# A gated linear-attention layer and its feed-forward on one core: the hand-kept list of 1,629 steps is written in another order

## The chip, the core and the metric

The kernel runs on 1 core of one Trainium2 chip. The measure is the device time of one execution in microseconds (us). The core has five instruction streams: TensorE (PE, whose weight loads are shown apart as PEld), VectorE (DVE), ScalarE (ACT), GpSimd (POOL) and SyncE (SP, which only issues transfers here). Each takes its own instructions strictly in the order written, and waits for the others through semaphores.

## What is computed

The first half is a recurrent attention with an exponential input gate and a forget gate, over 4 batches, 8 heads, 768 positions and 40 values a head. The second half is a two-layer feed-forward with a piecewise activation, over all 3,072 positions, 320 wide with 2,048 hidden units.

```python
for t in range(S):
    m_new = np.maximum(f_gate[:, :, t] + m, i_gate[:, :, t])
    f_stab = np.exp(f_gate[:, :, t] + m - m_new)
    i_stab = np.exp(i_gate[:, :, t] - m_new)
    C = f_stab * C + i_stab * einsum('bhd,bhe->bhde', vt, kt)
    n = f_stab * n + i_stab * kt
    h_tilde = einsum('bhde,bhe->bhd', C, qt)
    denom = np.maximum(np.abs(einsum('bhd,bhd->bh', n, qt)), 1.0)
    y[:, :, t] = sigmoid(o_gate[:, :, t]) * h_tilde / denom
h = y @ w_in
g = np.where(h >= 1, h, np.where(h <= -1, 0.0, (h + 1) ** 2 / 4))
out = g @ w_out
```

All inputs and the output are 32-bit floats. The matrices of the feed-forward are split into a high and a low part, so that several products of narrower words make up one exact enough product.

## The kernel before

Time is cut into 6 chunks of 128 positions. With 4 batches that makes 24 attention pieces, numbered n = 0 to 23. The feed-forward works on 6 groups j of 512 positions (four pieces each) and 16 slices of 128 hidden units, so on 96 blocks numbered 16j + slice. A block can start when all four pieces of its group are done.

Everything after the set-up is driven by one string, `STEPS`, near the top of the file. A loop goes through its words and issues the instructions of each. The words that the text uses are:

- `fi`, `fb`, `qk.n`, `v.n`, `A.n`, `W.k`, `og.c` load (SP issues): gates, queries and keys, values, cumulated decays, weight block k, output gates of a chunk.
- `score.n` (PE, then two DVE products into the decay tile `Abc`), `prep.n` (a POOL selection, then two times four ACT exponentials on `Abc`), `carry.n` (the state `C`), `main.n` (the rest of a piece: products, normalization, `y`, a transpose by PE, and then the split copies `xh`, on ACT, and `xl`, on DVE).
- `mm.x`, `relu.x`, `max.x`, `gh.x`, `gl.x`, `out.x`/`outh.x`/`outl.x`: the eight products of block x (PE), its activation (two ACT instructions `r`), the limit (DVE), the high part (ACT), the low part (DVE) and the second product (PE).
- `w.k`: the next part of the conversion of weight block k. The weights arrive as 64-bit words, and W.0 to W.15 are alternately blocks of the first matrix (`win`, even k) and of the second (`ow`, odd k). The word `w.k` stands five to seven times in the list, and each time one instruction of the block is issued: two on ACT (`mg<-wraw`, then `win<-wraw` or `ow<-wraw`), three on DVE (`mg<-mg`, then `win<-wraw` or `ow<-wraw`, then `win<-mg,win` or `ow<-mg,ow`). Even blocks go on with a cast `wh<-win` on ACT and the rest `wl<-win,wh` on DVE. For odd blocks the word `so.i` does the same later (`oh<-ow` on ACT).
- `hot.k`: k products on zeros, to keep PE busy; `sig.c`: the sigmoid of a chunk, which needs another table on ACT (ACT_TABLE_LOAD before and after).

The conversion of a block begins like this; `mg` is one buffer for all blocks, and so is the `win` tile of the even ones:

```python
mg = stage.tile([P, n], F32, name="mg", bufs=1)
nc.scalar.activation(mg, hi.bitcast(F32), AF.Abs, scale=65536.0)
yield
out = new().rearrange("p k f -> p (k f)").bitcast(I32)
...
nc.vector.tensor_scalar_max(mg, mg, TINY)
yield
...
nc.vector.scalar_tensor_tensor(out=out, in0=mg.bitcast(I32), scalar=3, in1=out,
```

So the first ACT instruction of block k+1 waits until the fifth instruction of block k (the third on DVE, `ow<-mg,ow` or `win<-mg,win`) has read `mg`. The blocks of the first feed-forward group (x = 0 to 15) need the weights in step with their numbers: `mm.x` needs both parts of W.k with k = x or x - 1, whichever is even.

The list decides the order of every engine's instructions, and with it what stands ahead of what; nothing reorders them later. Two words in it, `--` and `++`, close the buffers of the gates and of the weight conversion and open others in their place.

Of the kernel before, what the change touches and what calls it, by code (L numbers as in the profile page):

```python
# [48 lines left out]
    "fi.0 mask.1 fb.0 W.0 vv.0 mask.0 hot.2 sums.0 mask.3 qk.1 add.1 hot.2 add.0 qk.2 w.0 w.0 bmax.0 id.0 dec.1.0 "  # L49
    "dec.1.1 dec.0.0 score.1 qk.3 gtail.0 hot.2 hot.2 bmax.0 gex.0 score.1 mask.2 w.0 qk.0 add.2 dec.2.0 dec.2.1 "  # L50
    "vv.2 add.3 w.0 v.4 dec.3.1 v1.1 dec.3.0 score.1 og.0 W.1 dec.0.1 score.2 main.1 score.0 bsum.0 bsum.0 bsum.0 "
    "w.0 score.3 score.2 score.2 one.0 score.0 v.1 score.0 v1.2 btail.0 w.0 v1.0 sig.0 main.1 btail.0 hot.4 "
    "btail.0 btail.0 w.0 v1.3 main.0 score.3 v.0 main.0 W.2 hot.2 exps.0 main.0 main.1 main.2 hot.2 hot.2 qn.5 A.4 "
    "score.3 v2.4 main.2 main.2 main.0 w.1 v2.1 qk.4 main.0 w.1 w.1 cs.0 main.3 main.1 main.2 main.0 W.3 v.5 "
    "carry.4 main.3 main.3 hot.2 v2.0 qn.4 main.1 w.1 decs.0 main.1 v.2 w.1 carry.1 main.3 A.5 A.6 main.2 w.2 "
    "carry.0 main.2 main.3 main.3 prep.4 carry.0 w.2 v1.4 w.2 mm.0 mm.1 prep.4 v2.5 w.2 W.4 w.2 -- prep.4 qk.6 "
    "carry.1 w.2 score.4 w.3 w.2 w.3 relu.1 main.4 main.4 mm.3 v2.2 prep.5 qk.5 w.3 carry.5 score.4 W.5 relu.0 W.6 "
    "relu.3 w.3 score.4 carry.5 max.1 prep.6 w.3 mm.2 main.5 relu.2 w.4 max.0 max.2 main.4 carry.2 decs.0 main.4 "
    "out.0 v.3 og.1 v.6 max.3 w.4 qn.6 v1.5 prep.6 carry.4 prep.5 w.4 so.0 W.7 w.4 w.5 main.5 w.4 out.1 A.7 "
    "score.5 w.4 carry.5 carry.2 score.5 w.5 main.4 w.5 w.4 v.7 score.6 prep.6 out.2 mm.4 carry.4 w.5 prep.5 "  # L60
    "score.6 w.6 w.6 sig.1 mm.5 w.5 score.5 w.6 v1.6 W.8 main.5 w.6 v2.6 relu.5 w.6 w.6 main.6 v2.3 W.9 out.3 w.7 "
    "qn.7 score.6 qk.7 carry.5 prep.7 main.5 relu.4 main.4 max.5 w.7 w.6 prep.7 main.6 main.6 W.10 carry.6 w.8 "
    "max.4 main.6 v1.7 qn.8 carry.6 mm.6 carry.3 W.11 w.8 w.7 relu.6 w.7 w.7 mm.7 relu.7 out.4 carry.4 carry.3 "
    "main.7 main.5 W.12 w.8 w.8 W.13 main.5 w.8 v2.7 max.6 main.4 max.7 main.7 out.5 main.4 w.9 w.9 w.8 prep.7 v.8 "
    "main.4 W.14 w.9 w.9 score.7 carry.6 out.6 w.10 carry.6 so.1 w.9 v.9 w.10 w.8 mm.9 score.7 relu.9 w.10 w.10 "
    "mm.8 qn.9 score.7 w.10 w.10 w.11 w.11 relu.8 main.6 main.7 max.9 w.10 w.12 A.8 w.11 mm.10 w.11 w.11 qk.8 A.9 "
    "W.15 main.6 max.8 w.12 w.12 mm.11 relu.11 w.12 so.5 w.12 carry.7 out.7 w.12 main.7 w.13 so.5 w.12 qk.9 mm.13 "
    "w.13 max.11 relu.10 w.13 w.13 main.5 gh.11 w.13 w.14 max.10 main.5 gl.11 v2.8 carry.7 gh.10 main.7 out.8 "
    "mm.12 w.14 A.11 w.14 prep.8 relu.13 w.14 relu.12 prep.8 gl.10 main.5 out.9 v1.8 prep.8 max.12 w.14 prep.9 "
    "w.14 max.13 outh.10.0.1 outh.10.2.3 outl.10 main.6 so.6 main.7 w.15 main.6 score.8 w.15 score.8 outh.11.0.1 "  # L70
    "outh.11.2.3 outl.11 score.8 w.14 w.15 w.15 gh.12 so.6 qn.11 w.15 ++ gh.13 main.8 main.8 main.6 mm.14 prep.9 "
    "qk.10 relu.14 mm.15 og.2 main.7 gl.12 so.2 main.8 gl.13 outh.12.2.3 qk.10 main.7 relu.15 main.8 max.14 main.9 "
    "lg.0 main.7 gh.14 A.10 outh.12.0.1 so.7 outl.12 stack.10 so.1 outh.13.2.3 main.8 outh.13.0.1 carry.7 mm.17 "
    "main.8 outl.13 so.7 qk.11 max.15 mm.16 main.8 main.9 relu.17 gh.15 prep.9 v1.9 score.9 max.17 gl.14 gl.15 "
    "stack.10 relu.16 main.8 gh.17 outh.14.2.3 outh.14.0.1 prep.10 outl.14 mm.19 outh.15.0.1 stack.10 sig.2 "
    "carry.7 gl.17 main.8 qn.10 mm.20 outh.15.2.3 max.16 gh.16 outl.15 main.9 relu.19 prep.10 stack.10 mm.18 "
    "carry.8 score.9 main.8 gl.16 score.9 sto.0.2 sto.0.0 mm.22 max.19 carry.8 relu.20 main.9 v.10 score.10 so.0 "
    "relu.18 sto.0.3 main.8 main.9 max.20 v2.9 sto.0.1 qk.11 main.9 mm.21 main.10 A.12 score.10 max.18 so.2 "
    "prep.11 relu.22 main.10 so.4 main.9 main.8 outh.16.2.3 outh.16.0.1 outl.16 prep.10 carry.8 so.3 qn.13 "
    "outh.17.0.1 gh.18 max.22 outh.17.2.3 main.8 prep.11 stack.11 gh.20 score.10 gh.19 v1.10 outl.17 so.4 carry.9 "  # L80
    "gl.18 relu.21 outh.18.2.3 outh.18.0.1 carry.8 carry.9 stack.11 carry.9 v.11 main.10 outl.18 gl.20 v2.10 qk.12 "
    "mm.25 main.10 gl.19 relu.25 outh.19.0.1 main.9 outh.19.2.3 mm.23 outl.19 max.21 outh.20.2.3 gh.22 so.3 "
    "outh.20.0.1 prep.12 main.10 max.25 gh.21 gl.21 carry.9 mm.24 carry.10 stack.11 outl.20 main.9 stack.12 "
    "relu.23 prep.12 relu.24 main.9 prep.11 main.10 outh.21.2.3 v.12 qk.12 stack.11 qn.12 max.23 outh.21.0.1 "
    "carry.10 outl.21 score.11 main.11 A.13 v2.11 main.10 score.11 mm.27 max.24 outh.22.0.1 stack.12 main.10 "
    "score.11 prep.12 gh.24 main.10 gh.23 gl.22 relu.27 mm.31 v1.11 mm.28 relu.31 g5.5 gl.23 main.11 main.10 qk.14 "
    "main.11 outh.22.2.3 main.11 qk.13 gl.24 gh.25 carry.10 mm.26 outl.22 outh.23.0.1 max.31 main.10 relu.26 "
    "max.27 outh.23.2.3 stack.12 main.11 main.12 stack.14 prep.13 outl.23 outh.24.2.3 outh.24.0.1 A.14 main.11 "
    "gl.25 outl.24 max.26 main.9 main.12 qk.13 og.3 stack.14 relu.28 max.28 main.11 carry.10 main.11 outh.25.0.1 "
    "mm.29 stack.12 v1.12 gh.27 gh.26 main.9 outh.25.2.3 gl.27 main.12 carry.11 v.13 relu.29 gl.26 main.9 main.11 "  # L90
    "outl.25 stack.13 outh.26.2.3 mm.30 v.14 prep.13 main.12 outh.26.0.1 A.15 gh.28 carry.11 score.12 main.11 "
    "outl.26 v2.12 relu.30 max.29 gl.28 qk.15 score.12 outh.27.2.3 score.12 main.12 outh.27.0.1 main.11 carry.12 "
    "outl.27 max.30 main.10 outh.28.2.3 prep.13 carry.11 outh.28.0.1 main.10 main.11 stack.13 qk.15 stack.13 "
    "main.13 main.12 outl.28 main.11 gh.29 mm.35 main.13 relu.35 qn.14 gh.30 gh.31 mm.34 carry.11 main.12 stack.13 "
    "gl.30 carry.12 v1.13 gl.29 outh.29.0.1 mm.32 outh.29.2.3 relu.34 outl.29 outh.30.0.1 main.13 max.35 gh.35 "
    "main.13 relu.32 main.12 stack.15 v2.13 max.32 outh.30.2.3 max.34 outl.30 gh.32 outh.31.2.3 gl.31 score.13 "
    "mm.33 score.13 mm.39 score.13 main.12 outh.31.0.1 outl.31 relu.33 qk.14 stack.15 gl.32 prep.14 g5.5 gl.35 "
    "carry.12 main.13 prep.14 carry.12 max.33 carry.13 mm.36 mm.38 main.13 carry.13 sto.1.3 relu.39 g5.5 sto.1.0 "
    "relu.36 main.14 qk.16 A.16 gh.33 main.13 max.36 carry.13 v.15 sig.3 mm.41 stack.14 prep.15 outh.32.0.1 "
    "outh.32.2.3 sto.1.1 g5.5 gl.33 relu.41 outl.32 main.13 qn.15 max.39 mm.37 sto.1.2 stack.15 outh.33.0.1 "  # L100
    "stack.14 outh.33.2.3 main.13 gh.34 qk.16 gh.39 main.13 stack.15 relu.37 outl.33 gl.34 main.12 v1.14 gh.36 "
    "outh.34.0.1 gl.39 max.41 qk.17 prep.14 outh.34.2.3 main.14 outl.34 outh.35.0.1 qn.17 score.14 max.37 qn.16 "
    "outh.35.2.3 qk.17 score.14 gl.36 stack.16 v.16 A.17 relu.38 outl.35 carry.13 main.14 g5.5 score.14 gh.37 "
    "outh.36.2.3 mm.43 outh.36.0.1 main.15 v2.14 carry.14 mm.40 outl.36 v2.15 outh.37.2.3 stack.16 max.38 main.14 "
    "score.15 gh.38 outh.37.0.1 gl.37 outl.37 prep.15 main.12 carry.14 main.14 main.15 outh.38.2.3 g5.5 score.15 "
    "relu.40 carry.14 outh.38.0.1 gl.38 A.18 main.14 prep.15 max.40 qn.19 outl.38 prep.16 v.17 stack.16 qk.18 "
    "outh.39.2.3 g5.5 outh.39.0.1 main.12 main.13 main.12 score.15 stack.17 v1.15 stack.17 main.14 main.13 gh.40 "
# [922 lines left out]
```

## Time and profile before

| | |
|---|---|
| time before, median of 3 runs | 471.26 us (469.88 to 471.52) |
| span of the profiled execution, from first to last instruction | 467.8 us |
| the profiled execution's own time beside its span | not recorded; the median of the runs is 3.5 us above the span |
| PE busy | 458.4 us, 98% of the span, 3312 matmuls |
| DVE, ACT, POOL busy | 359.8 us (77%), 326.0 us (70%), 150.5 us (32%) |
| chain of work that ended last | PE 94%, DVE 2%, DMA 1% |
| transfers | 60.60 MB, mean 130 GB/s |

The table is read as follows: PE has hardly any idle time in this execution, while DVE and ACT have a quarter to a third over the whole span, but not in each stage of it. A matmul is shown as busy until its modelled end, and consecutive ones overlap.

### The profile page before, as it was taken

Reading aid. Unit: us, or ns where it says so; the run is one execution under the profiler, and the core shown is the slowest. Engines: PE = TensorE matmul, PEld = TensorE weight load, DVE = VectorE, ACT = ScalarE, POOL = GpSimd, SP = SyncE. Lnnn points to the kernel's source line nnn. Section 1 sums busy time; section 2 is a strip of 40 time slices with the busy share of each in tenths; the row PEclk is TensorE's granted clock in tenths of the full one; section 3 lists DMA queues with packets and bytes.
Section 4 is the critical chain, followed back from the end, with each engine's and each line's share of the span. In section 5 each row is a group of like instructions: output and inputs, shape, how many; then the busy total and the mean of one; then the engine's idle time right before and its main releaser. Section 6 shows DMA issues by size and latency. Waiting matters only on the chain.

```text
span 467.8 us, 8768 instructions
## 1 busy us (share of the span) xinstructions
PE 458.4 (98%) x3312; PEld 407.1 (87%) x3312; DVE 359.8 (77%) x651; ACT 326.0 (70%) x587; POOL 150.5 (32%) x153
## 2 busy tenths in 40 slices
PE   6999999999999999999999999999999999999997
PEld 3888787788899999889899989999899989888996
DVE  5888888999989889698998988887578875343342
ACT  3578898998987556588675986766596735544561
POOL 2265042133454554332543433452243240000000
PEclk9999999999999999999999999999999999999999
DMA  6899955656452534526234654424533000001001
GB/s 219 281 288 324 331 177 186 202 194 160 116 177 70 175 89 154 138 80 202 76 117 149 169 150 128 128 70 138 157 100 115 2 1 1 1 0 57 0 1 56
DMA packets 24552, 60.60 MB, mean 130 GB/s; under 512 B 2599, under 2 KB 12607, under 8 KB 24511
## 3 DMA queue, kind: packets, MB, share of 16 engines
q1 hardware_dynamic: 24223, 59.81, 41.8%
q8 instruction: 26, 0.43, 0.4%
q10 hardware_dynamic: 288, 0.25, 0.2%
q14 instruction: 15, 0.12, 0.1%
HBM read 55.96 MB, written 4.01 MB: 128 GB/s over the span
## 4 chain that ended last, share of the span: by engine, by line
PE 94%; DVE 2%; DMA 1%; SPq 1%; ACT 1%; issue 0%; DVEq 0%
PE ps L191 94%; DMA raw<-in_qk 1%; DVE gl L191 1%; SPq L191 1%; DVE ow L191 1%; ACT r L191 0%; DVE wl L191 0%; DVE Abc L191 0%; ACT oh L191 0%; DVE z L191 0%; DVE r L191 0%; ACT xh L191 0%; SPq L188 0%; DVE y L191 0%; DVE xh L191 0%
## 5 line engine op out<-in xcount | busy, mean ns | idle before, releaser
L191 PE MATMUL ps<-oh,gh 128*128 128x320 f32 x344 | 105.6, 317 | 0.0
L191 ACT ACTIVATE r<-ps,half 128x512 f32<-128x512 f32 x96 | 65.6, 684 | 56.1 <-PE ps L191 41.6
L191 PE MATMUL ps<-ow,gh 128*128 128x320 f32 x344 | 103.0, 309 | 0.0
L191 PE MATMUL ps<-xh,wh 128*128 128x512 f32 x288 | 100.6, 403 | 0.8 <-ACT xh L191 0.8
L191 PE MATMUL ps<-xh,wl 128*128 128x512 f32 x288 | 98.3, 395 | 0.3 <-DVE wl L191 0.3
L191 DVE TENSOR_TENSOR gl<-r,gh 128x512 fp32r<-128x512 f32 x86 | 65.7, 770 | 38.2 <-ACT gh L191 35.6
L191 DVE SCALAR_TENSOR_TENSOR r<-ps,r 128x512 f32<-128x512 f32 x96 | 65.1, 684 | 24.1 <-ACT r L191 23.9
L191 ACT CAST gh<-r 128x512 fp32r<-128x512 f32 x86 | 52.0, 613 | 38.9 <-PE ps L191 32.2
L191 PE MATMUL ps<-oh,gl 128*128 128x320 f32 x344 | 66.0, 312 | 1.0 <-DVE gl L191 1.0
L191 PEld LDWEIGHTS ps<-oh,gh 128*128 128x128 f32 x344 | 64.6, 188 | 2.2 <-ACT o L191 0.2
L191 PEld LDWEIGHTS ps<-ow,gh 128*128 128x128 f32 x344 | 64.8, 188 | 1.8
L191 PEld LDWEIGHTS ps<-xh,wl 128*128 128x128 f32 x288 | 54.0, 188 | 13.5 <-DVE wl L191 0.7
L191 ACT ACTIVATE r<-r 128x512 f32<-128x512 f32 x96 | 60.7, 633 | 3.0
L191 PE MATMUL ps<-xl,wh 128*128 128x512 f32 x192 | 60.3, 395 | 0.0
L191 PEld LDWEIGHTS ps<-xh,wh 128*128 128x128 f32 x288 | 50.3, 188 | 8.2 <-ACT xh L191 1.0
L191 PEld LDWEIGHTS ps<-oh,gl 128*128 128x128 f32 x344 | 54.3, 188 | 2.5 <-DVE gl L191 1.2
L191 POOL TENSOR_TENSOR v<-vk,G 128x328 f32<-128x328 f32 x36 | 30.7, 855 | 70.3 <-PE ps L191 40.5
L191 ACT ACTIVATE Abc<-Abc,nA 128x128 f32<-128x128 f32 x160 | 50.4, 390 | 3.4 <-POOL Abc L191 3.3
L191 POOL TENSOR_TENSOR y<-y,z 128x320 f32<-128x320 f32 x24 | 22.9, 957 | 77.3 <-DVE y L191 75.0
L191 POOL TENSOR_TENSOR m<-m 128x1024 bf16<-128x1024 f32 x16 | 32.9, 2053 | 40.8 <-DVE m L191 38.6
L191 PEld LDWEIGHTS ps<-xl,wh 128*128 128x128 f32 x192 | 36.0, 188 | 8.8
L191 DVE SCALAR_TENSOR_TENSOR stk<-raw,ident,qs 120x1024 fp32r<-120x1024 f32 x28 | 37.0, 1326 | 1.1 <-ACT raw L191 1.0
(146 smaller groups left out, 711.1 us busy)
## 6 DMA issues: line engine op xcount, KB each, us to landing
qs<-in_qs SPq DMA_DIRECT2D x28, 480.0 KB
Abc<-a_d SPq DMA_DIRECT2D x20, 512.0 KB
vk<-in_vk SPq DMA_DIRECT2D x20, 324.0 KB
wraw<-in_w_in SPq DMA_DIRECT2D x8, 768.0 KB
wraw<-in_w_out SPq DMA_DIRECT2D x8, 640.0 KB
sig<-in_og SPq DMA_DIRECT2D x6, 640.0 KB
qn<-in_qn SPq DMA_DIRECT2D x20, 180.0 KB
raw<-in_qk SPq DMA_DIRECT2D x20, 160.0 KB
```

The costliest lines, as they stand in the source:

```text
L191: r = getattr(self.engine, name)(*args, **kwargs)
```

## The change

`STEPS` is replaced by another order of the same 1,629 words. Every word stands in both lists equally often, so operations, buffers, pools and inputs are the same; the marks `--` and `++` stand at other places in the list (words 139 and 407 before, 115 and 418 after). Two lines of each list, from the stretch in which W.1 to W.4 are converted:

```diff
-    "carry.0 main.2 main.3 main.3 prep.4 carry.0 w.2 v1.4 w.2 mm.0 mm.1 prep.4 v2.5 w.2 W.4 w.2 -- prep.4 qk.6 "
-    "carry.1 w.2 score.4 w.3 w.2 w.3 relu.1 main.4 main.4 mm.3 v2.2 prep.5 qk.5 w.3 carry.5 score.4 W.5 relu.0 W.6 "
+    "decs.0 so.0 A.6 carry.1 w.2 w.2 v2.0 A.5 qk.5 carry.0 carry.0 w.2 w.2 W.5 mm.0 mm.1 w.2 w.2 prep.4 relu.0 v2.5 "
+    "main.4 main.4 v2.2 w.2 score.4 prep.4 score.4 qk.6 main.5 main.5 W.6 max.0 carry.5 w.3 w.3 prep.4 score.4 "
```

The first place is ACT's row from the first transposed copies (`xh`) to the conversion of W.3. `mg` and `win` at 128x768 are W.2's two parts, `wh` its cast; `mg` and `ow` at 128x640 are W.3's; `r` is an activation and `Abc` an exponential of `prep.4`. Before:

```order
L191 CAST xh<-ps 128x3x128
L191 ACTIVATE mg<-wraw 128x768
L191 CAST xh<-ps 128x3x128
L191 ACTIVATE win<-wraw 128x768
L191 ACTIVATE Abc<-Abc,nA 128x128 x8
L191 CAST wh<-win 128x3x256
L191 ACTIVATE mg<-wraw 128x640
L191 ACTIVATE ow<-wraw 128x640
L191 ACTIVATE r<-ps,half 128x512
L191 ACTIVATE r<-r 128x512
```

The same place after the change (`oh` is `so.0`, the cast of W.1):

```order
L190 CAST oh<-ow 128x640
L190 ACTIVATE mg<-wraw 128x768
L190 ACTIVATE win<-wraw 128x768
L190 CAST wh<-win 128x3x256
L190 ACTIVATE r<-ps,half 128x512
L190 ACTIVATE r<-r 128x512
L190 ACTIVATE Abc<-Abc,nA 128x128 x4
L190 ACTIVATE mg<-wraw 128x640
L190 ACTIVATE ow<-wraw 128x640
L190 ACTIVATE Abc<-Abc,nA 128x128 x4
```

Eight exponentials stood between `win` and `wh` and now nothing does; `oh` now stands ahead of W.2, and an activation and four exponentials stand ahead of W.3.

The second place is ACT's row at the conversion of W.12 (the parts at 128x768) and the start of W.13's (at 128x640). Before:

```order
L191 ACTIVATE mg<-wraw 128x768
L191 ACTIVATE win<-wraw 128x768
L191 ACTIVATE r<-ps,half 128x512
L191 ACTIVATE r<-r 128x512
L191 CAST oh<-ow 128x640
L191 CAST wh<-win 128x3x256
L191 ACTIVATE mg<-wraw 128x640
L191 ACTIVATE ow<-wraw 128x640
```

After:

```order
L190 ACTIVATE mg<-wraw 128x768
L190 ACTIVATE win<-wraw 128x768
L190 CAST oh<-ow 128x640
L190 ACTIVATE r<-ps,half 128x512
L190 ACTIVATE r<-r 128x512
L190 CAST xh<-ps 128x3x128
L190 ACTIVATE r<-ps,half 128x512
L190 ACTIVATE r<-r 128x512
L190 CAST wh<-win 128x3x256
L190 ACTIVATE mg<-wraw 128x640
```

One more activation and one `xh` copy stand ahead of W.12's cast, and so ahead of W.13.

## Rows read from the trace of the kernel before

**Rows 1.** The page: the span, and PE's busy time, its share and instructions.

```profile
span 467.8 us, 8768 instructions
PE 458.4 (98%) x3312; PEld 407.1 (87%) x3312; DVE 359.8 (77%) x651; ACT 326.0 (70%) x587; POOL 150.5 (32%) x153
```

**Rows 2.** PE's waits: line, waited for, us in total, times, longest.

```profile
PE ps L191 <- DMA raw<-in_qk: 1.5, 2, 0.9
PE ps L191 <- DVE gl L191: 1.0, 1, 1.0
PE ps L191 <- ACT xh L191: 0.8, 1, 0.8
PE ps L191 <- DVE wl L191: 0.3, 1, 0.3
```

**Rows 3.** Busy time by engine (instructions), 26 to 116 us; then clock, DMA share, GB/s.

```profile
26.00:116.00 90.00, 88.91 (x540) 73.67 (x539) 80.47 (x146) 77.90 (x139) 30.70 (x32) 1.00 0.74 233
```

**Rows 4.** Instructions on tile mg: min/median/max ns, first and last start us.

```profile
L191 ACT ACTIVATE mg<-wraw x15: 787/813/925, 25.1 to 103.2; 128x640 f32<-128x640 f32 x8, 128x768 f32<-128x768 f32 x7
...
L191 DVE SCALAR_TENSOR_TENSOR ow<-mg,ow x8: 803/826/1281, 29.7 to 106.4; 128x640 int32<-128x640 int32 x8
```

**Rows 5.** ACT, 26 to 116 us by form: busy us, mean ns | idle before.

```profile
L191 ACT ACTIVATE Abc<-Abc,nA 128x128 f32<-128x128 f32 x44 | 13.6, 389 | 0.0
L191 ACT ACTIVATE r<-ps,half 128x512 f32<-128x512 f32 x17 | 11.5, 674 | 4.4 <-PE ps L191 4.4
L191 ACT ACTIVATE r<-r 128x512 f32<-128x512 f32 x17 | 10.7, 631 | 0.5
L191 ACT ACTIVATE win<-wraw 128x768 uint16<-128x768 uint16 x7 | 7.6, 1089 | 0.0
L191 ACT ACTIVATE ow<-wraw 128x640 uint16<-128x640 uint16 x8 | 7.4, 926 | 0.0
L191 ACT ACTIVATE mg<-wraw 128x768 f32<-128x768 f32 x7 | 6.3, 907 | 3.9 <-DVE ow L191 3.8
L191 ACT CAST wh<-win 128x768 fp32r<-128x768 f32 x7 | 5.8, 824 | 0.8 <-DVE win L191 0.8
L191 ACT ACTIVATE mg<-wraw 128x640 f32<-128x640 f32 x7 | 5.6, 796 | 0.7 <-DVE win L191 0.7
L191 ACT CAST oh<-ow 128x640 fp32r<-128x640 f32 x6 | 4.3, 718 | 0.0
L191 ACT CAST xh<-ps 128x384 fp32r<-128x384 f32 x8 | 3.8, 472 | 1.7 <-PE ps L191 1.6
...
L191 ACT ACT_TABLE_LOAD x2 | 2.6, 1283 | 0.0
L191 ACT ACTIVATE sig<-sig 128x1280 f32<-128x1280 f32 x1 | 1.3, 1270 | 0.0
```

**Rows 6.** DVE, the same window and columns: the parts of the weight conversion.

```profile
L191 DVE SCALAR_TENSOR_TENSOR ow<-mg,ow 128x640 int32<-128x640 int32 x8 | 7.0, 879 | 0.3
...
L191 DVE SCALAR_TENSOR_TENSOR win<-mg,win 128x768 int32<-128x768 int32 x7 | 6.7, 955 | 0.3
L191 DVE TENSOR_SCALAR win<-wraw 128x768 uint16<-128x768 uint16 x7 | 5.4, 775 | 0.0
L191 DVE TENSOR_SCALAR mg<-mg 128x768 f32<-128x768 f32 x7 | 4.8, 689 | 0.4 <-ACT mg L191 0.4
L191 DVE TENSOR_SCALAR ow<-wraw 128x640 uint16<-128x640 uint16 x8 | 4.6, 569 | 0.0
...
L191 DVE TENSOR_SCALAR mg<-mg 128x640 f32<-128x640 f32 x8 | 4.2, 527 | 0.0
```

**Rows 7.** ACT in order of time from 25 us: start, length [idle before].

```profile
25.89 0.48 ACT L191 CAST xh<-ps 128x384 fp32r<-128x384 f32 x1
26.27 0.93 ACT L191 ACTIVATE ow<-wraw 128x640 uint16<-128x640 uint16 x1
```

**Rows 8.** SP's issue of transfers in order of time: start, length of the issue.

```profile
1.19 0.70 SPq L191 DMA_DIRECT2D fi_r<-in_fi  x1
```

223 rows, old and new, of the table STEPS are left out of this document.

## The prediction

> **What bounds the kernel now.** I read the page's busy times first. PE is busy for 458.4 of 467.8 us [rows 1], and the reader is to see that a reordering alone cannot take away more than the 9.4 us that are left. Next I read PE's waits. Of those on other engines and on transfers, four groups stand out: 1.5 us for the first queries and keys, 1.0 for a `gl`, 0.8 for an `xh` and 0.3 for a `wl` [rows 2]. That is 3.6 us in all, the most that a better order has to win in the places that the profile names. So the old list runs near PE's pace, and the question is what the new one makes PE wait for.
>
> Then I looked for a stage in which the other engines have little to spare. From 26 to 116 us DVE is busy for 80.5 and ACT for 77.9 of 90 us, with the clock of PE at full (1.00) [rows 3]. This is where the weights are converted. The view of the tile `mg` shows the conversion as one thread: W.1's first instruction starts at 25.1 us, W.15's fifth at 106.4 and takes about 0.8, so it ends at 107.2 [rows 4]. It lasts 82.1 us. Since `mg` is one buffer, no block may begin before the fifth part of the block ahead, so the parts form a serial chain that goes from ACT to DVE and back. ACT stood still 3.8 us for that reason [rows 5].
>
> Taken alone, the parts of one block last, on the even blocks, 0.907 + 1.089 + 0.689 + 0.775 + 0.955 = 4.4 us, on the odd ones 0.796 + 0.926 + 0.527 + 0.569 + 0.879 = 3.7 us [rows 5, 6]. For 7 even and 8 odd blocks this is 60.4 of the 82.1 us. Only 21.7 us of other work and waiting lay on that thread in the old order.
>
> **The change, part by part.** *The conversion.* The first pair of rows of the order shows the pattern. Before, W.2's `win` and `wh` had eight exponentials between them, so ACT worked while DVE did W.2's three parts. After, nothing stands between them and ACT waits. The work that filled the gap (an activation, four exponentials, the cast `oh`) now stands ahead of the next block's first part, so it adds to the thread. The second pair shows the same at W.12, with one activation more ahead of the cast and of W.13.
>
> I followed the new order back from the last use of the converted weights through whatever stands immediately ahead in its engine's row, or through the producer when that ends later. Of the 75 parts of W.1 to W.15, 57 are on this chain (beside the others an engine has longer work): the first ACT part 7 times odd and 5 even, the second 7 and 5, DVE's first 8 and 3, second 8 and 3, third 8 and 3. With the means of rows 5 and 6 that is 5.57 + 4.54 + 6.48 + 5.45 + 4.22 + 2.07 + 4.55 + 2.33 + 7.03 + 2.87 = 45.1 us. To it come:
> - 6 casts `wh` at 0.824 and 3 `oh` at 0.718: 7.1 us [rows 5].
> - 8 activations of two instructions, 0.674 + 0.631: 10.4 us [rows 5].
> - 20 exponentials. They overlap, and 13.6 us of busy time over 44 makes 0.309 each: 6.2 us [rows 5].
> - `sig.1` with its two table loads, 1.270 + 2 × 1.283: 3.8 us [rows 5].
> - One `xh` copy, 0.5 us [rows 5].
> - 26 further DVE instructions of the attention. The window's DVE time without the conversion's six forms is 80.47 - 32.7 = 47.8 us over 146 - 45 = 101 instructions, 0.473 each: 12.3 us [rows 3, 6].
> - 7 on POOL (selections and products) at 30.70 / 32 = 0.96: 6.7 us [rows 3].
>
> The sum is 92.1 us. Neighbours on one engine overlap: an `xh` copy from 25.89 lasts 0.48, and the next instruction starts at 26.27, 0.10 early [rows 7]. Over some 95 such neighbours I take off 0.065 each (an estimate between nothing and the 0.10 of that pair), 6.2 us; for some 35 passes from engine to engine I add 0.035 each, an estimate, 1.2 us. That leaves 87.1 us against the 82.1 before: **+5.0 us**. The bounds are 92.1 (no overlap at all, +10.0) and, with the full 0.10 and free passes, 82.6 (+0.5).
>
> What hides this? Nothing, I think: PE waits for `wl` and `xh` in just this stage already [rows 2], so a thread that ends later moves the first products of W.12 and W.14, then the second group's blocks, by as much. Behind it PE has no idle time in which to catch up; what it loses stays lost.
>
> At one point of this sum the notes on the chip put another price. In the rows the table load takes 1.283 us, and the two instruction forms that follow such loads show 0.0 us of idle time ahead [rows 5]. The Trainium skill (ScalarE: Activation LUTs, What ACT_TABLE_LOAD costs) states for each switch the same 1.283 us and a drain of about 1.38 us on top. By it the two switches on the chain would cost 2.8 us more and the sum would be +7.8; the trace does not show the drain.
>
> *The start.* The new list issues `fb`'s two loads ahead of `fi`, so the first gate arithmetic comes later by their issue, of which one takes 0.70 us [rows 8]; the queries and keys for the first products are ahead of the weights instead of behind them. PE lost 1.5 us there before [rows 2]. The two work against each other, and I take 0, with bounds of -1.5 (that wait is gone, and the gates' lateness stays covered by products on zeros and masks) and +1.4 (two issues of that length, with nothing else to do).
>
> *The middle and the end.* From about 116 us on, the new order keeps PE's operations and mixes them otherwise. DVE and ACT have slack there, and before, PE's named wait in that part was 1.0 us for a `gl` [rows 2]. I take 0, between -1.0 (that wait goes) and +2.0 (two more like it). The last four stores change places, which I take as 0: the same copies and issues stand behind the last product.
>
> The sum is +5.0 us: the span goes to 472.8 and, with the 3.5 us that the median of the runs lies above this profile's span, the time to **476.3 us**.
>
> **The rivals.** *The lengthening is hidden, no change.* If the overlap is as large as the lower bound, the thread lasts 82.6 us, and 471.8 us is the time. For it speaks that some of the chain's members could be started earlier than my following back allows; against it, that ACT and DVE are 87 and 89% busy in the stage [rows 3]. I give it 0.16.
>
> *Faster.* The new order removes the named waits: the start's transfers come in time (-1.5) and the waits for `gl`, `xh` and `wl` (-2.1) are gone [rows 2], while the thread stays as it is. That gives 467.7 us. It decides from the point where the conversion thread of the new order ends before 107 us. The stage's load speaks against it. I give it 0.12.
>
> *Much slower.* The thread's parts overlap less and the passes cost more, so it takes the upper +10.0, which gives 481.3 us; or the single buffers make the transfers of later weight blocks wait for their places, which has the same price by the same buffers. What speaks for it is that all 35 passes from engine to engine are priced at an estimated 0.035 us. I give it 0.14.
>
> *A costlier table switch.* If each of the two switches on the chain held ACT up for as long again as its load, 1.283 us [rows 5], the chain would be 2.6 us longer and the time 478.9 us. The idle column of rows 5 speaks against it; 0.05, and it lies in the forecast's own range. The drain that the Trainium skill states (ScalarE: Activation LUTs, What ACT_TABLE_LOAD costs) would be such a hold-up, and by its figure the time would be 479.1 us.
>
> **How the numbers follow.** The forecast has 0.53, with its own range of 473.7 to 480. The whole range is 470 to 482 us: it takes in the hidden case and the upper bound, and leaves out the faster case and what is beyond +10.7. Half a per cent, 2.4 us, is about what a measurement of this kernel can tell from no change. Faster by more than that (below 468.9) has 0.11; within it (468.9 to 473.6) 0.18, mostly the hidden case; slower (above 473.6) 0.71, from the forecast, the upper case and the costlier switch.
>
> **What the profile will show.** If I am right, the first `mg` instruction of W.1 and the last `ow<-mg,ow` of W.15 lie about 87 us apart instead of 82; PE's waits for `wl`, `wh`, `xh` and `gl` grow from 2.1 us to about 7, nearly all between 35 and 120 us; PE's busy time stays within 1 us of 458.4; ACT shows more idle time ahead of `wh` released by DVE's `win`, and DVE more ahead of `mg` released by ACT. After 120 us the two traces run at one distance. I am wrong if the thread is no longer than 83 us, if PE waits chiefly for transfers, or if the distance grows or shrinks by more than 2 us after 120 us.

## The result and the profile after

The changed kernel takes 472.61 us (median of 10 runs), the kernel before 470.00 us (median of 10 runs beside them). The ratio is 1.0072, with a 95% interval of 1.0044 to 1.0101: slower by 3.4 us (2.1 to 4.7), where 5.0 were forecast. Some executions of most lists, the old one too, are some 6 to 12 us longer, at a lower mean granted clock of PE (the ratio leaves out two such of the old list, at 481.7 and 481.9 us); times given below "at full clock" are medians over the executions with a mean granted clock of at least 0.998, and by these it is 472.1 against 469.8 us (the old list's 54 such executions beside the experiments). The two spans differ by 2.2 us.

The sign and roughly the size are as forecast, the place is not. The page of the changed kernel, to be held against [rows 1]:

```profile
span 470.0 us, 8761 instructions
PE 459.5 (98%) x3309; PEld 408.4 (87%) x3312; DVE 360.3 (77%) x651; ACT 326.3 (69%) x587; POOL 156.1 (33%) x153
```

PE's waits, which answer to [rows 2]:

```profile
PE ps L187 <- DMA raw<-in_qk: 6.3, 1, 6.3
PE ps L190 <- DMA raw<-in_qk: 0.4, 1, 0.4
PE ps L190 <- POOL v L190: 0.2, 1, 0.2
```

The waits for `wl`, `xh` and `gl` have not grown, they are gone. In their place stands one wait of 6.3 us, for the queries and keys of piece 1, at the very start. [rows 2] leaves out what stood there before, the longest of all PE's waits: 2.2 us for POOL, ahead of the first product. PE in order of time, first in the kernel before (start, length, [idle before and its cause]):

```profile
2.18 0.58 PE L188 MATMUL ps<-late_t,idb 128*128 128x512 bf16 x1 [2.18 <-POOL rst L188]
...
8.88 0.46 PE L191 MATMUL ps<-raw 40*128 40x128 f32 x2 [0.93 <-DMA raw<-in_qk]
9.91 1.13 PE L191 MATMUL ps<-raw 40*128 40x128 f32 x14 [0.58 <-DMA raw<-in_qk]
```

and in the changed kernel:

```profile
6.26 0.79 PE L187 MATMUL ps<-raw 40*128 40x128 f32 x2 [6.26 <-DMA raw<-in_qk]
7.42 2.08 PE L190 MATMUL ps<-raw 40*128 40x128 f32 x14 [0.37 <-DMA raw<-in_qk]
9.42 1.89 PE L190 MATMUL ps<-late_t,idb 128*128 128x512 bf16 x4
...
17.98 2.06 PE L190 MATMUL ps<-raw 40*128 40x128 f32 x32
```

In the old list PE's first products are the masks of `mask.1` (`late_t`, `idb`), which need nothing from a transfer, so they fill the time until the queries and keys land. In the new list the products of `score.1` stand ahead of the masks, and PE takes its products in the order of the list: the masks, which began at 2.18 us before, stand behind the scores and begin at 9.42 us. In both traces PE's first products run at about half rate (three masks in 1.49 us before, four in 1.89 after, where two take 0.59 later); after the change the scores are among them, and the 14 products take 2.08 us instead of 1.13. The trace's record of the granted clock begins only with the upper of its two levels (2.4 GHz), at 5.0 us before and at 13.1 us after the change; the 1.00 that the rows below show for the time ahead of that is no reading.

The stages add up as follows. Busy time by engine, the kernel before (the stage from 26 to 116 us is [rows 3]; PE is the first number behind the length, DVE the third):

```profile
0.00:26.00 26.00, 22.18 (x190) 16.16 (x190) 19.00 (x58) 13.74 (x21) 8.17 (x23) 1.00 0.80 258
...
116.00:232.00 116.00, 115.51 (x899) 105.20 (x897) 101.32 (x173) 87.54 (x161) 51.48 (x46) 1.00 0.45 129
232.00:350.00 118.00, 117.51 (x932) 107.88 (x933) 97.20 (x165) 84.75 (x157) 47.32 (x42) 1.00 0.43 128
```

The changed kernel:

```profile
0.00:26.00 26.00, 19.32 (x156) 13.97 (x158) 17.16 (x44) 12.06 (x16) 6.20 (x19) 1.00 0.63 191
26.00:116.00 90.00, 89.58 (x551) 74.23 (x552) 78.81 (x155) 76.24 (x138) 30.43 (x33) 1.00 0.75 245
116.00:232.00 116.00, 116.00 (x903) 106.08 (x902) 103.46 (x180) 88.69 (x164) 55.77 (x48) 1.00 0.47 134
232.00:350.00 118.00, 118.00 (x968) 107.73 (x967) 99.17 (x165) 83.55 (x153) 49.07 (x43) 1.00 0.45 125
```

Idle time of PE up to 26 us: 26 - 22.18 = 3.8 us before, 6.7 after, a loss of 2.9. From 26 to 350 us: 1.1 + 0.5 + 0.5 = 2.1 before, 0.4 after, a gain of 1.7. PE's busy time grew by 459.5 - 458.4 = 1.1 us; those 14 products at half rate alone take 0.95 us more. Together 2.9 - 1.7 + 1.1 = 2.3, against 2.2 between the spans. So in this profile the new start costs about 4 us, if all of the added busy time belongs to it, and the rest of the new order wins some of it back.

The conversion, on which the forecast rested, shows no longer thread. The changed kernel's tile `mg` and the start of W.1 (answering to [rows 4]):

```profile
L190 DVE SCALAR_TENSOR_TENSOR ow<-mg,ow x8: 817/824/944, 33.9 to 110.3; 128x640 int32<-128x640 int32 x8
```

```profile
29.60 0.79 ACT L190 ACTIVATE mg<-wraw 128x640 f32<-128x640 f32 x1
```

From 29.6 to 110.3 + 0.8 = 111.1 us it lasts 81.5 us, 82.1 before and 87.1 in my sum. It begins 4.5 us later, behind the late start. It also holds nothing up: the chain of work that ended last, followed back from the end, stays in PE's row from 35.5 to 466.6 us, where before it went through work on the converted weights (`oh` on ACT, `ow` and `wl` on DVE) from 88.9 to 91.3 us.

```profile
35.51 79.62 PE ps L190 x472
115.18 351.39 PE ps L190 x2609
```

### The profile page after: what moved, and what is told of

Its sections match the earlier page's. It is cut to its first block, busy times and chain, and to the rows that moved or that the text cites. A ratio compares the mean times of both kernels' runs of the same rounds, so it can differ in the third digit from the quotient of the medians.

```text
span 470.0 us, 8761 instructions
## 1 busy us (share of the span) xinstructions
PE 459.5 (98%) x3309; PEld 408.4 (87%) x3312; DVE 360.3 (77%) x651; ACT 326.3 (69%) x587; POOL 156.1 (33%) x153
## 4 chain that ended last, share of the span: by engine, by line
PE 97%; DMA 1%; SPq 0%; POOL 0%; DVE 0%; issue 0%; ACT 0%; POOLq 0%
PE ps L190 97%; DMA raw<-in_qk 1%; SPq L190 0%; POOL y L190 0%; SPq L187 0%; POOL v L190 0%; DVE z L190 0%; ACT r L190 0%; DVE y L190 0%; POOLq L190 0%
## 5 line engine op out<-in xcount | busy, mean ns | idle before, releaser
L190 PE MATMUL ps<-oh,gh 128*128 128x320 f32 x344 | 104.2, 313 | 0.0
L190 DVE TENSOR_TENSOR gl<-r,gh 128x512 fp32r<-128x512 f32 x86 | 64.5, 764 | 24.9 <-ACT gh L190 21.9
L190 ACT CAST gh<-r 128x512 fp32r<-128x512 f32 x86 | 52.0, 614 | 39.3 <-PE ps L190 22.5
L190 POOL TENSOR_TENSOR y<-y,z 128x320 f32<-128x320 f32 x24 | 21.9, 915 | 89.0 <-DVE y L190 89.0
L190 POOL TENSOR_TENSOR v<-vk,G 128x328 f32<-128x328 f32 x36 | 33.2, 926 | 45.4 <-PE ps L190 23.9
L190 DVE SCALAR_TENSOR_TENSOR stk<-raw,ident,qs 120x1024 fp32r<-120x1024 f32 x28 | 41.4, 1479 | 1.6 <-ACT raw L190 1.5
L190 DVE TENSOR_TENSOR Abc<-ps,Abc 128x512 f32<-128x512 f32 x46 | 30.6, 683 | 8.2 <-ACT Abc L190 5.3
```

Source lines behind the costliest of these rows:

```text
L190: r = getattr(self.engine, name)(*args, **kwargs)
```

## The experiments

Three theories stood against each other. **Start theory**: the place of `score.1` ahead of the masks makes the loss. **Conversion theory**, that of the prediction. **Gate theory**: the gates, loaded second instead of first, delay the start.

**The two halves apart.** The old list's first 37 words, then the new order (of this and the other lists only the words at the place of the edit are shown; `...` stands for what follows or lies between):

```diff
-fb.0 fi.0 sums.0 bmax.0 qk.1 score.1 mask.2 mask.0 add.0 dec.0.0 mask.1 ...
+fi.0 mask.1 fb.0 W.0 vv.0 mask.0 hot.2 sums.0 mask.3 qk.1 add.1 ...
```

> The first 37 words of the old list, then the other words in the new order. Start theory (the whole loss is made before 13 us, because PE's first products wait for queries and keys until 6.26 us, and the new order of the rest wins back about 2.2 us): PE begins at 2.2 us, the lead at the start is 4.4 us, and the time is about 2.2 us under that of the kernel before, a ratio of 0.995, span near 465.6 us. Conversion theory (the prediction: the new order of the weight conversion costs 5 us and the start nothing): no shorter than the changed kernel, 2 to 5 us above the kernel before, ratio 1.005 to 1.01, with W.1 to W.15 taking about 87 us.

The median is 470.71 us, ratio 1.0022 (0.9985 to 1.0059), with five of the 12 executions some 6 to 8 us longer by a fall of the clock; the three at full clock have 468.8 us, 1.0 under the kernel before. The other way round, the new list's first 36 words and then the old order:

> The first 36 words of the new list, then the other words in the old order. Start theory: PE begins at 6.3 us and never catches up; about 4 us above the kernel before, ratio 1.008 to 1.010, span near 472, since the old order of the rest keeps its own waits of 2.2 us. Conversion theory: the conversion stands in the old order, so the time is that of the kernel before within 1 us, ratio 1.000.

It takes 473.07 us, ratio 1.0068 (1.0050 to 1.0086): the new start alone costs 3.2 us, although the conversion of W.1 to W.15 stands in the old order. PE's waits there are 6.4 us for the queries and keys and then the old ones again (1.0 for `gl`, 0.8 for `xh`, 0.5 for `wl`). The conversion theory falls.

**One cause in the start.** The old list with the load `qk.1` and the first `score.1` moved ahead of the masks, and `fb.0` ahead of both:

```diff
-fi.0 mask.1 fb.0 W.0 vv.0 mask.0 hot.2 sums.0 mask.3 qk.1 add.1 ...
+fi.0 fb.0 qk.1 score.1 mask.1 W.0 vv.0 mask.0 hot.2 sums.0 mask.3 add.1 ...
```

> The old list with four words put in another order at its head: fi.0 fb.0 qk.1 score.1 mask.1, so that PE's first products are those of score.1, whose load is issued at 2.6 us as in the changed kernel, and everything behind stays as before. Start theory (the place of score.1 ahead of the masks alone makes the loss): PE begins at about 6.3 us and the time rises by 2.5 to 3.5 us, ratio 1.005 to 1.0075. If the loss of the new start comes from the rest of its order (late gates, late first conversion): within 1 us of the kernel before, ratio under 1.002.

It takes 475.38 us, ratio 1.0113 (1.0099 to 1.0126), 5.3 us more, and its first products read

```profile
5.41 0.80 PE L187 MATMUL ps<-raw 40*128 40x128 f32 x2 [5.41 <-DMA raw<-in_qk]
8.01 2.07 PE L190 MATMUL ps<-raw 40*128 40x128 f32 x14 [1.80 <-DMA raw<-in_qk]
```

The place of `score.1`, even with its load issued earlier than in the old list, is enough for the whole loss, and for 2 us more than the new start has: the second half of the same load came 1.8 us late here. The gates alone:

```diff
-fb.0 fi.0 sums.0 bmax.0 qk.1 score.1 ...
+fi.0 fb.0 sums.0 bmax.0 qk.1 score.1 ...
```

> The new list with its first two words exchanged: the load fi stands ahead of the two loads of fb again, as in the old list. Gate theory (the gates arrive 2.35 us later in the new order and everything behind them too): the time falls by about 2.3 us to a ratio of 1.002. Start theory: PE's first products wait for queries and keys whose issue does not move, so the time stays within 0.7 us of the changed kernel, ratio 1.006 to 1.008.

472.66 us, ratio 1.0076 (1.0039 to 1.0112), as the changed kernel. The gate theory falls.

**The repair, and the clock.** The new list with the masks ahead of the scores:

```diff
-... qk.1 score.1 mask.2 mask.0 add.0 dec.0.0 mask.1 add.1 ...
+... qk.1 mask.2 mask.0 mask.1 score.1 add.0 dec.0.0 add.1 ...
```

> The new list with one word moved: the products of score.1 stand behind the six mask products instead of ahead of them, so that PE has work from 2.2 us on. Start theory: the six products (1.3 us at full clock, 2.6 at half) run while the queries and keys are under way; the time falls by 1.3 to 2.9 us against the changed kernel, to a ratio of 0.999 to 1.004 against the kernel before. Conversion theory: no change, ratio 1.007. Gate theory (the late load of the gates is what delays PE): no change either, 1.007.

This came out wrong by all three theories: 477.00 us, ratio 1.0140 (1.0109 to 1.0171). Its profile shows why. PE's row, and the stages (the last three numbers are the granted clock, the transfers' share and GB/s):

```profile
14.85 2.06 PE L190 MATMUL ps<-raw 40*128 40x128 f32 x32
```

```profile
14.00:22.00 8.00, 7.95 (x88) 6.47 (x86) 7.68 (x18) 6.92 (x9) 2.62 (x4) 1.00 0.77 232
22.00:24.00 2.00, 2.00 (x14) 2.00 (x14) 1.48 (x7) 0.56 (x1) 0.00 (x0) 0.63 1.01 393
24.00:36.00 12.00, 11.78 (x55) 11.09 (x55) 6.37 (x21) 3.49 (x8) 5.43 (x8) 0.50 0.97 308
36.00:38.00 2.00, 1.95 (x15) 1.60 (x16) 1.61 (x3) 0.86 (x2) 2.00 (x3) 0.96 0.51 178
```

At the 32 products of the scores PE was 17.98 - 14.85 = 3.1 us ahead of the changed kernel, more than the start theory says, since PE's full rate came at 5.4 us here and at 13.1 there. Then the granted clock fell to 0.50, the lower of its two levels (1.2 GHz), from 22.5 to 36.2 us, and in 13.7 us at half rate PE does 6.8 us less. PE was not idle before the fall: from 14 to 22 us it is busy for 7.95 of 8.00 us, in the second half of it on products of 128 columns over 40 rows and of 41 columns. The same products run in the changed kernel's profile from 21.4 us on, at a granted clock of 1.00. All six executions show a mean granted clock of 0.986 or less. To see whether products on zeros between them help, I dealt out the four of `hot.4`, once with the old head and once with the repaired new one:

```diff
-... dec.3.1 dec.3.0 hot.4 v.0 ...
+... dec.3.1 dec.3.0 hot.2 v.0 ...
...
-... main.1 main.1 main.0 main.0 ...
+... main.1 main.1 hot.2 main.0 main.0 ...
```

> As e1_start_old, with four of the zero products dealt out: two stay at their place ahead of piece 3's scores, two go between the products of main.1 and of main.0 (both 41 wide), which the new list put next to each other. Clock theory (in e1 the granted clock fell to half at the end of some 5 us of scores and 41-wide products without a wide one, and that cost 6 us): the fall at 22.7 us is gone from the profile and from most executions, and the time is 468.8 us, ratio 0.998. If the fall has nothing to do with the place of these products: half of the executions still show it, at about 475 us, ratio 1.002 as e1.

> As e3_masks_first (the changed kernel with the masks ahead of score.1's products), with the four zero products dealt out as in e5_old_split. Start theory with clock theory: the start's loss is gone and the fall too, 468.8 us, ratio 0.998, 3.3 us under the changed kernel. Start theory wrong: 472 us or more, ratio 1.005. Clock theory wrong: 474.7 us or more again, ratio 1.010 to 1.014.

The first has 476.68 us, since four of its six executions show a fall (two without it have 468.3, too few for an interval). The clock theory as I put it did not hold: the time forecast from it came in two of six. The four have a mean clock of 0.981 or 0.982, against 0.986 in e1's and e3's profiles; the profile is of an execution without a fall, so where theirs lie is not known. The second has 470.70 us, ratio 1.0020 (1.0008 to 1.0033), no such fall in 12 executions: it is 2.4 us under the changed kernel by the ratios and 1.3 at full clock, less than the 3.3 expected. In its profile the products run at half rate up to 14 us, where e3's, in the same order, were at full rate from 5.8 us on, and the 32 scores come at 16.83. So of the 3.1 us above 2.0 go with the rate at the start, which the mean clock does not show, and 1.2 with the order. With six more products on zeros behind the old head:

```diff
-... main.1 main.1 main.0 main.0 main.0 exps.0 main.1 hot.2 main.2 ...
+... main.1 main.1 hot.4 main.0 main.0 main.0 exps.0 main.1 hot.4 main.2 ...
```

> As e1_start_old with six more products on zeros among the 41-wide products (four between main.1 and main.0, and the pair ahead of main.2 made four), 1.3 us of PE time. Clock theory (the long row of scores and 41-wide products without wide ones is where the granted clock falls): no fall to half at 22 to 26 us, 468.8 + 1.3 = 470.1 us, ratio 1.001, in nearly every execution. If wide products there do not matter: about half of the executions again 6 us longer, as in e1 and e5.

470.70 us, ratio 1.0016 (1.0006 to 1.0026), with two of 12 executions at 479 us. A mean granted clock under 0.99 came in 2 of 10 executions of the changed list, 5 of 12 (e1), none of 6 (e2), 6 of 6 (e3), 3 of 9 (e4), 4 of 6 (e5), none of 12 (e6), 1 of 12 (e7), 1 of 10 (e8), none of 4 (e9), 3 of 12 (e10), 1 of 6 (e11), 2 of 12 here, and 13 of the 70 of the old list beside these runs, of which no profile shows the place. What decides it stays open.

**An earlier load.** The old head of e5 with one load moved up:

```diff
-fi.0 mask.1 fb.0 W.0 vv.0 mask.0 hot.2 sums.0 mask.3 qk.1 add.1 ...
+fi.0 mask.1 fb.0 qk.1 W.0 vv.0 mask.0 hot.2 sums.0 mask.3 add.1 ...
```

> As e5_old_split, and the queries and keys of piece 1 are loaded ahead of the first weight block and values instead of behind them. Start theory: PE's wait for them, 1.5 us in the kernel before, falls by up to the 0.95 us of the two issues that they pass; 467.9 us, ratio 0.996. If the landing is set by the transfers under way and not by the issue: 468.8 us, as e5.

470.84 us, ratio 1.0023 (1.0014 to 1.0032). The wait for the load is gone, and another has taken its place:

```profile
7.89 1.16 PE L190 MATMUL ps<-raw 40*128 40x128 f32 x16
11.62 0.86 PE L190 MATMUL ps<-zeros 128*128 128x512 bf16 x3 [2.56 <-ACT Abc L190]
```

ACT's exponentials of the decay (`Abc`) stand behind W.0's first two parts on ACT, and W.0 now lands later; PE's next product needs the buffer that they read. Behind this wait the granted clock was at its lower level from 12.4 to 15.8 us (the third number from the right):

```profile
12.00:14.00 2.00, 1.84 (x8) 0.87 (x8) 1.35 (x3) 0.81 (x3) 0.46 (x1) 0.61 0.48 140
14.00:16.00 2.00, 2.00 (x15) 1.41 (x13) 1.71 (x4) 0.92 (x2) 1.10 (x2) 0.54 0.99 256
```

Ten of the 12 executions have the same mean clock as this one, 0.996. The one at full clock has 470.3 us, so the fall is not the whole of what e7 is above e5's two executions at full clock (468.3).

**What the conversion's thread costs.** The old list, with one instruction of the conversion issued twice:

```diff
-        nc.scalar.activation(mg, hi.bitcast(F32), AF.Abs, scale=65536.0)
+        for _ in range(reps):
+            nc.scalar.activation(mg, hi.bitcast(F32), AF.Abs, scale=65536.0)
```

> The kernel before (old list) with the first ACT instruction of the conversion, mg<-wraw, issued twice for W.1 to W.6: 3 x 0.80 + 3 x 0.91 = 5.1 us more on the conversion's thread between 25 and 68 us; the result is the same. The prediction's step (PE has no cover, what the thread loses PE loses): 4 to 5 us above the kernel before, ratio 1.009 to 1.011. Cover theory (the thread has time to spare ahead of the products that use the weights, and ACT has idle time): under 1.5 us, ratio under 1.003, with PE's waits for wl, wh and xh under 2 us.

471.48 us, ratio 1.0043 (1.0025 to 1.0061), 1.5 us more at full clock for 5.1 us of work (`reps` is 2 for W.1 to W.6). On the other engine:

```diff
-        nc.vector.tensor_scalar_max(mg, mg, TINY)
+        for _ in range(reps):
+            nc.vector.tensor_scalar_max(mg, mg, TINY)
```

> The kernel before (old list) with DVE's first part of the conversion, mg<-mg, issued twice for W.1 to W.8: 4 x 0.53 + 4 x 0.69 = 4.9 us more, this time on DVE's row; the result is the same. In e8_stretch 5.1 us on ACT cost 1.6. DVE theory (from 26 to 116 us it is DVE's row as a whole that sets the pace of the conversion, so ACT's parts have cover and DVE's have not): 3 to 5 us above the kernel before, ratio 1.006 to 1.010, PE's waits for wl, gl and xh up by that. General cover theory (both engines have time to spare ahead of PE): 1.6 us or less, ratio under 1.004.

472.59 us, ratio 1.0057 (1.0044 to 1.0070), 2.5 us more at full clock for 4.9 us of work (W.1 to W.8): between the two theories. The tile `mg` (first and last start) and a wait of PE with ACT's instruction doubled:

```profile
L190 ACT ACTIVATE mg<-wraw x21: 780/817/936, 24.1 to 104.3; 128x640 f32<-128x640 f32 x11, 128x768 f32<-128x768 f32 x10
...
L190 DVE SCALAR_TENSOR_TENSOR ow<-mg,ow x8: 802/823/1280, 30.1 to 108.3; 128x640 int32<-128x640 int32 x8
```

```profile
PE ps L190 <- ACT xh L190: 1.8, 1, 1.8
```

and the tile with DVE's doubled:

```profile
L190 ACT ACTIVATE mg<-wraw x15: 782/807/929, 25.7 to 106.9; 128x640 f32<-128x640 f32 x8, 128x768 f32<-128x768 f32 x7
...
L190 DVE SCALAR_TENSOR_TENSOR ow<-mg,ow x8: 806/824/1281, 32.4 to 110.8; 128x640 int32<-128x640 int32 x8
```

With the last part's 0.8 us the thread lasts 85.0 and 85.9 us instead of 82.1: of 5.1 us on ACT 2.9 reach it, of 4.9 on DVE 3.8. And PE loses less than the thread does. With ACT's doubled, 1.0 of its 1.5 us is the longer wait for `xh` (1.8 against 0.8 in [rows 2]), a copy that stands behind W.1's part in ACT's row and is no part of the thread. With DVE's doubled, the waits for `xh`, `wl` and `wh` grew by 0.3, 0.2 and 0.2 us, and one of 0.5 us for the decay tile on DVE came to them:

```profile
PE ps L190 <- DVE Abc L190: 0.5, 1, 0.5
```

PE's idle time from 26 to 116 us, 1.1 us before, is 2.4 us with ACT's doubled and 2.5 with DVE's:

```profile
26.00:116.00 90.00, 87.60 (x533) 72.57 (x533) 79.36 (x146) 80.93 (x142) 30.64 (x33) 1.00 0.72 230
...
26.00:116.00 90.00, 87.47 (x530) 71.43 (x530) 82.27 (x156) 75.88 (x137) 30.70 (x33) 1.00 0.69 222
```

So of the 1.5 us 1.3 are lost there, and of the 2.5 us 1.4; the rest is not traced to a wait. The second profile is of an execution whose clock was at the lower level from 12.0 to 15.4 us, ahead of W.1.

**A list that beats both.** The old list up to `mm.1` (133 words), then the new order:

> The old list up to the first two products of the feed-forward (133 words, PE at 33 us), then the other words in the new order. Start theory (all loss is made in the first 18 us and the new order of the rest is the better one): 1.0 to 1.5 us under the kernel before, ratio 0.997 to 0.998, PE's waits for gl and wl gone. Conversion theory (W.2 to W.15 in the new order cost up to 5 us): 2 us or more above the kernel before, ratio 1.004 or more.

469.25 us, ratio 0.9978 (0.9965 to 0.9992), 468.9 at full clock: 0.9 us under the kernel before (1.0 by the ratio) and 3.3 under the changed one. PE's waits:

```profile
PE ps L190 <- ACT xh L190: 0.8, 1, 0.8
PE ps L190 <- DMA raw<-in_qk: 0.5, 1, 0.5
PE ps L190 <- DMA qn<-in_qn: 0.3, 1, 0.3
```

The `gl` and `wl` waits of [rows 2] are gone with the new rest, and the old start keeps its own. New start +3.2 (e2) and new rest -1.0 (this list, and e1 at full clock, which is cut where e2 is) make +2.2, near the 2.3 that the changed kernel shows at full clock. In e2 the conversion's thread lasts 84.0 us in the old order, here 82.7 in the new one: its length moves by as much with the start as with its own order.

## Why the prediction was right and wrong

**Slower by 5.0: right in sign, and in size by luck.** Two terms were wrong in opposite directions. The time itself, 476.3 us, was 3.7 too high. 1.3 of that lie in the 3.5 us that I put above the span: the median of the old list's ten runs is 470.0, 2.2 above its span.

**The conversion, +5.0: wrong, the thread is 0.6 us shorter in the trace.** The step that failed is the following back "through whatever stands immediately ahead in its engine's row": the path of 87.1 us that it gave does not exist in the changed kernel, whose thread lasts 81.5 us, less than even the lower bound of 82.6. In the sum of 92.1 us, 50 lay on ACT (its parts 22.0, casts 7.1, activations 10.4, exponentials 6.2, the sigmoid 3.8, a copy 0.5) and 6.7 on POOL. Which of these members were too many is not settled. Followed back with the real starts, the thread gives DVE's row between 28 and 65 us, ACT's between 16 and 45 and POOL's up to 10, depending on how long an idle time must be (0 to 0.4 us) to be followed to the other engine; in the kernel before it is 42 to 45 and 37 to 40. The two engines have nearly the same load in the 90 us (DVE 80.5 before and 78.8 after, ACT 77.9 and 76.2), so that one of them alone sets the pace is not shown; e8 and e11, where either one's work lengthened the thread, speak against it. That what the new order put ahead of the parts on ACT took the place of waiting for DVE is a reading of the rows and not shown by an experiment. The `mg` and `wh` rows of ACT, 26 to 116 us (busy, mean ns | idle before), show no more waiting than [rows 5]:

```profile
L190 ACT ACTIVATE mg<-wraw 128x768 f32<-128x768 f32 x7 | 6.3, 907 | 2.2 <-DVE ow L190 2.2
...
L190 ACT CAST wh<-win 128x768 fp32r<-128x768 f32 x7 | 5.8, 821 | 1.8 <-DVE win L190 1.7
```

2.2 + 1.8 against 3.9 + 0.8. That "nothing" hides a longer thread was wrong too: in e8 and e11 the thread was 2.9 and 3.8 us longer, and 1.5 and 2.5 us were lost.

**The start, 0 between -1.5 and +1.4: wrong, +3.2** (e2), outside its bounds. The bounds counted the issues on SP and the old wait of 1.5 us, but not PE's own row. The order of PE shows `score.1` ahead of the masks in the new list; I priced the queries and keys as coming earlier and did not ask what covers the time until they land. That cover, six products on constants, had moved behind the wait. What of the 3.2 us is the wait and what the later rise to full rate is not parted.

**The middle and the end, 0 between -1.0 and +2.0:** e10 prices it together with the conversion's stage, at -1.0. In the changed trace the `gl` wait went, as the lower bound says, and PE's idle time from 116 to 350 us fell from 1.0 us to nothing; from 26 to 116 us it fell from 1.1 to 0.4.

**What the profile was to show:** of the signs named for being wrong, a thread of at most 83 us and PE waiting chiefly for a transfer both came. PE's busy time within 1 us of 458.4: 459.5, just missed. Past 116 us the distance shrank by 1.0 us (0.98 us of PE's idle time up to 350 us, then none).

**The rivals.** "Hidden" gave 471.8 us, nearer to the measured 472.6 than the forecast, and was right about a thread hardly longer; it had nothing for the start either. "Faster" described the rest of the list rightly in kind (the waits for `gl`, `xh` and `wl` went and the thread stayed as it was), though the rest won 1.0 us and not 2.1, and it failed by the start. "Much slower" did not come: no wait of PE for the conversion is left. The costlier table switch did not happen; ACT in the changed kernel around `sig.1`, whose two switches were on the chain:

```profile
63.10 0.63 ACT L190 ACTIVATE r<-r 128x512 f32<-128x512 f32 x1
63.74 1.28 ACT L190 ACT_TABLE_LOAD   x1
65.04 1.27 ACT L190 ACTIVATE sig<-sig 128x1280 f32<-128x1280 f32 x1
...
68.86 0.94 ACT L190 ACTIVATE ow<-wraw 128x640 uint16<-128x640 uint16 x1
69.82 1.28 ACT L190 ACT_TABLE_LOAD   x1
71.11 1.29 ACT L190 ACTIVATE Abc<-Abc,nA 128x128 f32<-128x128 f32 x4
```

Each of the two loads begins within 0.02 us of the end of the instruction ahead, and what follows it within 0.02 us of its own. The Trainium skill (ScalarE: Activation LUTs, What ACT_TABLE_LOAD costs) states a drain of about 1.38 us there, and the trace shows none.

## What to carry to other kernels

When an order is rewritten, read the first ten rows of the engine that bounds the kernel before anything else: work that needs no transfer belongs ahead of the first product that waits for one; where it was moved behind, it cost 3.2 us here (e2), and 5.3 in e9. A serial path over two engines was not found by taking the nearest neighbour in each row: it came out 5.6 us too long, and of a thread that really was longer only half to two thirds were lost. Doubling one instruction on it prices that at little effort. Two lists with the same words can be cut at a point and joined (the old one's head, the new one's rest), which prices each part and here gave a list 0.2% faster than the old one.

## What was not expected of the hardware

The granted clock of PE fell to 0.50 from 22.5 to 36.2 us (e3), behind and within a stretch in which PE was busy nearly all the time, mostly on products of few rows or columns. This cost some 6 us (477.0 us in e3, 470.7 in e6), more than the change itself. A drop in the mean clock came in some executions of most lists and not in others of the same list. A shorter fall, from 12.4 to 15.8 us, stands behind a wait of PE of 2.6 us in e7. At the start the granted clock reads 1.00, although the same 14 products take 2.08 us in one list and 1.13 in the other: the record has no entry before the upper level, at 5.0 us before and 13.1 after the change. That the later first product makes the later rise is not shown: e6 began at 2.2 us and reached the upper level at 13.8, and e3, with the same first products, at 5.4.
